# Top-k attention and highway layer: the 32nd value as a third group of the joint maximum, a third buffer for the rectified tile, scaling and reciprocal apart

## The chip, the cores and the metric

The kernel runs on one core of a Trainium2 chip. The metric is the time of the program on the device, in microseconds; lower is better. The core's engines are named as the profile names them: PE (TensorE, matmuls; PEld its weight loads), DVE (VectorE), ACT (ScalarE), POOL (GpSimd) and SP (SyncE, which here only issues transfers). Each engine works through its own queue in the order in which the program put it there.

## The reference

Attention in which each query keeps only its 32 best keys, and behind it a highway layer.

```python
def _attn_ref(q, k, v):                       # each (8, 8, 576, 64): batch, heads, sequence, head
    scores = scale * np.matmul(q, k.transpose(0, 1, 3, 2))
    kth = np.partition(scores, -top_k, axis=-1)[..., -top_k:-top_k + 1]      # top_k = 32
    scores = np.where(scores >= kth, scores, -1000000000.0)
    scores = scores - np.max(scores, axis=-1, keepdims=True)
    attn = np.exp(scores)
    attn = attn / (np.sum(attn, axis=-1, keepdims=True) + 1e-09)
    return np.matmul(attn, v)

def _moe_ref(x, w_h, w_t, b_t):               # x: (4608, 512), the heads side by side
    H = np.maximum(x @ w_h, 0.0)
    T = 1.0 / (1.0 + np.exp(-(x @ w_t + b_t)))
    return T * H + (1.0 - T) * x
```

## The kernel before

A unit is one block of 128 query rows of one head (the last 64 rows of two heads make one unit), with its 576 scores per row. Two units make a pair; there are 288 units, 144 pairs, 18 to a batch. `step(i)` writes down the work of one round of a software pipeline by hand, for 143 rounds; `begin()` fills the pipeline and `finish()` empties it and does the last pair. The order in which the lines stand there is the order in each engine's queue; between engines, waits are put in from what each instruction reads and writes.

The 32nd largest score of a row is found without sorting all 576:

- `scores` (L308 to L334, PE) makes a pair's scores in PSUM. `segments` (L352, DVE) takes the 8 largest of each of 6 segments of 96 scores into the tile `cand`, 12 instructions per pair.
- `refine` (L365 to L381, DVE) turns these 48 candidates per row into a threshold that has at least 24 scores at or above it. L365 and L367 make larger and smaller ones of neighbouring lists, L369 negates, L372 and L375 take 8 extremes each, L377 writes 8 values per row into column 1 of `cand`, and L381, the joint maximum, reduces columns 0 and 1 of `cand` together: its results are the row's largest score (`TOP`) and the threshold (`THR`) in the tile `wall`. `refine` is a generator: each `yield` is a place at which `step` puts other work between.
- `mask_count` (L396, ACT) counts the scores above the threshold in its accumulator `csum` and makes a mask; `mask_add` (L409, PE) adds the mask into PSUM, so that these scores drop out; `below` (L419, DVE) takes the 8 largest of what is left, into `wall` beside the threshold. The 32nd score is now one of 9 numbers per row (`NPK` = 9), the threshold and those 8, and the count says which.
- `hits` (L425, DVE) compares the count with 9 marks, `pick_a` (L435, POOL) multiplies the hits by the 9 numbers, and `pick_b` (L438, DVE) sums the products: one of 9 isn't zero, so the sum is the 32nd score (`KTH` in `wall`, kept two units further on).
- `biases` (L390, POOL) makes two biases from `wall`: the row's largest score for the exponential (L415, ACT), the 32nd for a rectifier of steep slope (L442, ACT), which gives a unit's cut. A pair's second unit is cut by POOL (L453) with a comparison. The masked products (L449 and L459, or L464 where POOL was given no cut; DVE) join cut and exponential, and a transpose by DMA (L480, SP) turns the result for the matmul with v (L493, PE).

In a step the queue of DVE has, for pairs i and i + 1: the segments' maxima of i + 1, `below` of i, L365, L367, `hits`, L369, L372 twice, L375 twice, `pick_b` of i, L377, masked product of the first unit of i - 1, L381, masked product of the second unit. ACT's mask of i + 1 (L396) needs L381.

When all heads of a block of query rows are done, `xs_copy` (L507, ACT) has put the sums over keys, with the row sums of the exponentials, into `xs`, and the highway layer of the block is cut into pieces that later steps take in. `norm` (L556, L557, DVE) adds 1e-9, scales by 2 and takes the reciprocal; it is called at the end of a step, behind the masked products. POOL multiplies (L562), a DMA casts and turns the block, `hh` projects it with the weights `w_h` (L521, PE), and its `evac` (L606, ACT) writes the rectified result into the tile `h2`, which the profile calls h. POOL makes s1 = h2 + x (L607), h2 = h2 - x (L608) and h2 = h2 * t (L621); then `do_add` (L691, POOL) issues a DMA that adds h2 to s1, and s1 is stored. `h2` comes from the pool `fpool`, which has two buffers for each of its tiles: the rectifier of one block waits until the DMA of two blocks ago has read its buffer. 38 blocks go this way; `finish()` does the last ones in another.

At the end a check of the whole run decides whether a slower branch, which sorts in full, has to redo the work; it isn't taken here.

Of the kernel before, what the change touches and what calls it, by code (L numbers as in the profile page):

```python
# [10 lines left out]
ALU = mybir.AluOpType  # L11
FP32 = mybir.dt.float32
# [6 lines left out]
NSEG = 6  # L19
# [7 lines left out]
def kernel(  # L27
# [10 lines left out]
    nc = tc.nc  # L38
# [38 lines left out]
    etpool = ctx.enter_context(tc.tile_pool(name="et", bufs=6))  # L77
    xpool = ctx.enter_context(tc.tile_pool(name="x", bufs=3))
    fpool = ctx.enter_context(tc.tile_pool(name="f", bufs=2))
    xps = ctx.enter_context(tc.tile_pool(name="xps", bufs=2, space=bass.MemoryType.PSUM))  # L80
    ops = ctx.enter_context(tc.tile_pool(name="ops", bufs=1, space=bass.MemoryType.PSUM))
    fps = ctx.enter_context(tc.tile_pool(name="fps", bufs=1, space=bass.MemoryType.PSUM))
# [12 lines left out]
    for jj in range(NPK):  # L95
        nc.vector.memset(pidx[:, jj : jj + 1], S - 2.0 * (TOP_K - jj))

    TOP, THR, KTH = 0, 1, NPK + 1
    wall = consts.tile([P, NU + 2, NPK + 2], FP32)
    fac = consts.tile([P, 2, 2], FP32)  # L100
    nc.vector.memset(fac[:, :, 0], -scale)
# [6 lines left out]
        nc.vector.memset(en[:, 0, :, 0:1], 3.0e38)  # L108
        ends.append(en)
    csum = consts.tile([P, NU], FP32)  # L110
    nc.vector.memset(wall[:, 0:2, KTH : KTH + 1], 0.0)

    def kth(u):
        return wall[:, u + 2, KTH : KTH + 1]
# [6 lines left out]

    cands = []
    for i in range(4):
        cand = consts.tile([P, 2, 8, 8], FP32, name=f"cand{i}")
        nc.vector.memset(cand[:, :, NSEG:, 0:1], -3.0e38)
        cands.append(cand)
    NM = 4
    masks = []
# [228 lines left out]
    def refine(g, cand):  # L357
        u0, u1 = pairs[g][0], pairs[g][1] + 1
        en = ends[g % NE]
        one = cand[:, :, 0:NSEG:2, :]  # L360
        two = cand[:, :, 1:NSEG:2, ::-1]
        high = cpool.tile([P, 2 * HALF], FP32, name="high")
        low = cpool.tile([P, 2 * HALF], FP32, name="low")
        neg = cpool.tile([P, 2 * HALF], FP32, name="neg")
        nc.vector.tensor_tensor(high[:].rearrange("p (s k r) -> p s k r", s=2, r=8), one, two, ALU.max)  # L365
        yield
        nc.vector.tensor_tensor(low[:].rearrange("p (s k r) -> p s k r", s=2, r=8), one, two, ALU.min)  # L367
        yield
        nc.vector.tensor_scalar(neg[:], high[:], -1.0, None, ALU.mult)  # L369
        yield  # L370
        for s in range(2):
            nc.vector.max(en[:, 0, s, 1:9], low[:, s * HALF : (s + 1) * HALF])  # L372
            yield
        for s in range(2):
            nc.vector.max(en[:, 1, s, 0:8], neg[:, s * HALF : (s + 1) * HALF])  # L375
            yield
        nc.vector.scalar_tensor_tensor(  # L377
            out=cand[:, :, :, 1], in0=en[:, 1, :, 0:8], scalar=-1.0, in1=en[:, 0, :, 0:8], op0=ALU.mult, op1=ALU.min
        )
        yield  # L380
        nc.vector.tensor_reduce(  # L381
            wall[:, u0:u1, TOP : THR + 1],
            cand[:, :, :, 0:2].rearrange("p s r k -> p s k r"),
            mybir.AxisListType.X,
            ALU.max,
        )
        yield

    def biases(g):
        return nc.gpsimd.tensor_tensor(be[:, g], wall[:, 2 * g : 2 * g + 2, TOP : KTH + 1 : KTH - TOP], fac[:], ALU.mult)  # L390

# [22 lines left out]
        return e  # L416

    def below(u, ps):
        nc.vector.max(wall[:, u, THR + 1 : KTH], ps)  # L419


    def hits(pair):
# [7 lines left out]
        )  # L430
        return hit

    def pick_a(pair, hit):
        u0, u1 = pair[0], pair[1] + 1
        nc.gpsimd.tensor_tensor(hit[:], hit[:], wall[:, u0:u1, THR:KTH], ALU.mult)  # L435

    def pick_b(pair, hit):
        nc.vector.tensor_reduce(wall[:, pair[0] + 2 : pair[0] + 4, KTH], hit[:], mybir.AxisListType.X, ALU.add)  # L438
# [109 lines left out]
    def ffn_pieces(b, qt, xs):  # L548
        nh, ng, w = shape_of(qt)
        st = dict(b=b, qt=qt, xs=xs)  # L550
        blocks.append(st)

        def norm():
            xs3 = xs[:, 0 : nh * DE].rearrange("p (h e) -> p h e", e=DE)
            rinv = cpool.tile([P, H], FP32, name="rinv")
            nc.vector.tensor_scalar(rinv[:, 0:nh], xs3[:, :, D], 1e-9, 2.0, ALU.add, ALU.mult)  # L556
            nc.vector.reciprocal(rinv[:, 0:nh], rinv[:, 0:nh])  # L557
            x = xpool.tile([P, dm], FP32, name="x")
            st["x"] = x

            def scaled(e):
                e.tensor_tensor(  # L562
                    x[:, 0:w].rearrange("p (h d) -> p h d", h=nh),
                    xs3[:, :, 0:D],
                    rinv[:, 0:nh].unsqueeze(2).to_broadcast([P, nh, D]),
                    ALU.mult,
                )
                if by_dma:
                    casts.append(cast)
                else:  # L570
                    ready.extend([xt, hh, tt])

            pool_work.append((scaled, w))

        by_dma = isinstance(b, int) and units[-1][0:2] > (b, qt + 2)

        def cast():
            xb = xpool.tile([P, dm], BF16, name="xb")
            nc.gpsimd.dma_start(xb[:, 0:w], st["x"][:, 0:w])
            return partial(turn, xb)  # L580

        def turn(xb):
            st["xT"] = fpool.tile([P, n_g, P], BF16, name="xT")
            nc.sync.dma_start_transpose(st["xT"][:, 0:ng, :], xb[:, 0:w])
            flying.append(b)
            ready.extend([hh, tt])

        def xt():
            ps = fps.tile([P, 512], FP32, tag="fp", name="fp")
            for g in range(ng):  # L590
                nc.tensor.transpose(ps[:, g * P : (g + 1) * P], st["x"][:, g * P : (g + 1) * P], ident_f[:])
            xT = fpool.tile([P, n_g, P], BF16, name="xT")
            st["xT"] = xT
            psv = ps[:].rearrange("p (g j) -> p g j", j=P)
            return lambda: nc.scalar.copy(xT[:, 0:ng, :], psv[:, 0:ng, :])

        def hh():
            ps = fps.tile([P, 512], FP32, tag="fp", name="fp")
            project(ps, qt, st["xT"], wh, False)
            h2 = fpool.tile([P, dm], FP32, name="h2")  # L600
            s1 = xpool.tile([P, dm], FP32, name="s1")
            st["h2"], st["s1"] = h2, s1
            x = st["x"]

            def evac():
                nc.scalar.activation(h2[:, 0:w], ps[:, 0:w], AF.Relu)  # L606
                pool_work.append((lambda e: e.tensor_add(s1[:, 0:w], h2[:, 0:w], x[:, 0:w]), w))  # L607
                pool_work.append((lambda e: e.tensor_sub(h2[:, 0:w], h2[:, 0:w], x[:, 0:w]), w))  # L608

            return evac  # L610

        def tt():
            ps = fps.tile([P, 512], FP32, tag="fp", name="fp")
            project(ps, qt, st["xT"], wt, True)
            if by_dma:
                flying.pop()
            t = fpool.tile([P, dm], FP32, name="tt")
            h2, s1 = st["h2"], st["s1"]

            def gated(e):  # L620
                ins = e.tensor_mul(h2[:, 0:w], h2[:, 0:w], t[:, 0:w])  # L621
                if e is nc.gpsimd:
                    adds.append((s1[:, 0:w], h2[:, 0:w], partial(store, b, qt, s1)))
                else:
                    e.tensor_add(s1[:, 0:w], s1[:, 0:w], h2[:, 0:w])
                    store(b, qt, s1)
                return ins

            def evac():
                nc.scalar.activation(t[:, 0:w], ps[:, 0:w], AF.Tanh)  # L630
                pool_work.append((gated, w))

            return evac

        return norm
# [21 lines left out]

    def blk_diff(k, ps):
        w = shape_of(k["qt"])[2]
        k["d"] = fpool.tile([P, dm], FP32, name="h2")  # L660
        nc.vector.scalar_tensor_tensor(
            out=k["d"][:, 0:w], in0=ps[:, 0:w], scalar=0.0, in1=k["x"][:, 0:w], op0=ALU.max, op1=ALU.subtract
        )
# [108 lines left out]
    def step(i):  # L772
# [75 lines left out]
        for _ in range(2):  # L848
            next(ra, None)
        if live:  # L850
            hit = hits(pr)
            pick_a(pr, hit)
        added = bool(adds or casts)
        if adds:
            do_add(i)
# [5 lines left out]
            todo_v.pop(0)()  # L861
        for _ in range(5):
            next(ra, None)
        if live:
            pick_b(pr, hit)
        next(ra, None)
        masked(0)
        for _ in ra:
            pass
        last = masked(1)  # L870
        if live:
            after(biases(i + 1), last)
        if norms:
            norms.pop(0)()
        if nxt:
            masks_of(i + 1)
        while turns and turns[0][0] <= i and len(flying) < 2:
# [61 lines left out]
    def finish():  # L939
# [49 lines left out]
        hit = hits(pr)  # L989
        ep, _ = keep_min(pu[0], old["e"][0], relu)  # L990
        old["et"][0] = transposes(ep)
        nc.vector.tensor_tensor(hit[:], hit[:], wall[:, pr[0] : pr[1] + 1, THR:KTH], ALU.mult)
        pick_b(pr, hit)
        x2 = xps.tile([P, 3 * BANK], FP32, tag="x", name="xs")
        cur["et"] = [etpool.tile([P, nck, P], BF16, name="et") for s in range(2)]
# [13 lines left out]
        yb = xs_of(nfull, 0, n)  # L1009
        project(bank(x1, 0), ya["qt"], ya["xT"], wh, False)  # L1010
        do_work(nc.vector, NG * dm)
        nc.vector.scalar_tensor_tensor(cond[:], wall[:, 0:NU, THR + 1], ABOVE, wall[:, 0:NU, THR], ALU.mult, ALU.add)
        while stores:
            stores.pop(0)[1]()
        sure(2, cond[:], 1.0)
# [28 lines left out]
    with tc.If(fine < 1):  # L1044
        with tc.For_i(0, B, 1) as bi:
# [26 lines left out]
            for pr in pairs[0 : NG // B]:  # L1072
# [23 lines left out]
                else:  # L1096
                    xs_copy(0, n, pso, xs, r0, r0 + P2)
                if heads[-1] == H - 1:
                    ffn_pieces(bi, qt, xs)()
                    do_work(nc.vector, NG * dm)  # L1100
                    while ready:
                        ready.pop(0)()()
                        do_work(nc.vector, NG * dm)
# [30 lines left out]
```

## Time and profile before

| | us |
|---|---|
| median of 3 runs | 817.38 (813.4 to 819.01) |
| the profiled execution | 818.4 |
| its span, first to last instruction | 816.7 |
| busy: DVE | 776.2 |
| busy: ACT | 758.8 |
| busy: PE | 694.4 |
| busy: POOL | 559.3 |
| DVE L352, segments' maxima, 1728 | 297.1 |
| DVE L419, the 8 largest below the threshold, 288 | 204.0 |
| DVE L449 and L459, masked products, 143 and 135 | 64.5 and 60.5 |
| DVE L381, joint maximum, 144 | 29.4 |
| DVE L438, sum over the hits, 144 | 21.8 |

The busy time of an engine counts an instruction from its start to its end; on DVE one starts a little before the one ahead of it has ended, so a group's time can be more than the room that it takes in the queue. Each group's line has the line of the code, the engine, the operation, the tile written and those read, the shapes, the number of instructions, their busy time, the mean duration of one in ns, and the idle time of the engine just ahead of them with what ended it. In a timeline the columns are start, duration (of all in the row, where "x12" says that it stands for 12), engine, line, operation and tiles; a bracket at the end gives the idle time just before and what ended it. "remote" as the end of a wait means that the profile doesn't tell what released it.

The granted TensorE clock is at 0.993 over the span.

### The profile page before, as it was taken

Reading aid. Unit: us, or ns where it says so; the run is one execution under the profiler, and the core shown is the slowest. Engines: PE = TensorE matmul, PEld = TensorE weight load, DVE = VectorE, ACT = ScalarE, POOL = GpSimd, SP = SyncE. Lnnn points to the kernel's source line nnn. Section 1 sums busy time; section 2 is a strip of 40 time slices with the busy share of each in tenths; the row PEclk is TensorE's granted clock in tenths of the full one; section 3 lists DMA queues with packets and bytes.
Section 4 is the critical chain, followed back from the end, with each engine's and each line's share of the span. In section 5 each row is a group of like instructions: output and inputs, shape, how many; then the busy total and the mean of one; then the engine's idle time right before and its main releaser. Section 6 shows DMA issues by size and latency. Waiting matters only on the chain.

```text
span 816.7 us, 20679 instructions
## 1 busy us (share of the span) xinstructions
PE 694.4 (85%) x6405; PEld 500.2 (61%) x6499; DVE 776.2 (95%) x4020; ACT 758.8 (93%) x1401; POOL 559.3 (68%) x712
## 2 busy tenths in 40 slices
PE   7889988888878888888888888888888888888884
PEld 5666766566655666566665666556656566565562
DVE  6999999999999999999999999999998999998995
ACT  5999999999999999999999998999999999998984
POOL 2666867777677766787667777677776776675750
PEclk9999999999999999999999999999999999999998
DMA  6799957985798657997679866697767975565553
GB/s 121 85 147 155 130 117 136 156 130 80 146 150 145 108 94 137 152 137 115 101 149 147 127 110 117 134 157 126 107 122 128 163 114 92 94 110 96 101 93 87
DMA packets 346359, 100.37 MB, mean 123 GB/s; under 512 B 330624, under 2 KB 338432, under 8 KB 346240
## 3 DMA queue, kind: packets, MB, share of 16 engines
q1 hardware_dynamic: 291024, 79.16, 53.0%
q0 software_dynamic: 53536, 19.34, 22.4%
q8 instruction: 53, 0.87, 0.4%
q10 hardware_dynamic: 1680, 0.46, 0.3%
q14 instruction: 66, 0.54, 0.2%
HBM read 31.72 MB, written 9.44 MB: 50 GB/s over the span
## 4 chain that ended last, share of the span: by engine, by line
ACT 37%; DVE 31%; PE 23%; DMA 4%; issue 3%; POOL 2%; SPq 0%; ACTq 0%; DVEq 0%; POOLq 0%
ACT m L396 14%; DVE wall L419 10%; DVE cand L352 9%; ACT e L415 7%; PE pso L277 6%; ACT sc L347 6%; ACT r L442 4%; PE xs L325 4%; DVE ep L449 3%; PE xs L308 3%; PE pso L493 2%; ACT xs L507 2%; DMA s<-h 2%; PE xs L409 2%; PE fp L521 2%
## 5 line engine op out<-in xcount | busy, mean ns | idle before, releaser
L352 DVE MAX8 cand<-xs 128x8 f32<-128x96 f32 x1728 | 297.1, 246 | 13.4 <-PE xs L334 7.4
L277 PE MATMUL pso<-cst,ident_b 128*128 128x252 bf16 x1881 | 253.1, 274 | 42.4 <-ACT xs L507 40.0
L453 POOL TENSOR_SCALAR ro<-sc,wall 128x576 bf16<-128x576 f32 x135 | 232.6, 1723 | 0.0
L277 PEld LDWEIGHTS <-ident_b 128*128 128x128 bf16 x1881 | 178.1, 98 | 82.1 <-issue 49.1
L415 ACT ACTIVATE e<-sc,be 128x576 bf16<-128x576 f32 x288 | 226.0, 785 | 0.1
L419 DVE MAX8 wall<-xs 128x8 f32<-128x576 f32 x288 | 204.0, 748 | 11.5 <-PE xs L409 5.0
L308 PE MATMUL xs<-kT,qT 64*128 64x256 f32 x1024 | 146.1, 402 | 31.9 <-DVE high L365 28.3
L347 ACT COPY sc<-xs 128x1152 f32<-128x1152 f32 x144 | 160.8, 1116 | 0.7 <-DVE cand L352 0.6
L308 PEld LDWEIGHTS xs<-kT,qT 64*128 64x128 f32 x1024 | 93.5, 187 | 62.9 <-issue 38.1
L435 POOL TENSOR_TENSOR hit<-hit,wall 128x18 f32<-128x18 f32 x143 | 32.4, 226 | 137.0 <-DVE hit L425 129.4
L396 ACT ACTIVATE m<-xs,wall 128x576 int8<-128x576 f32 x144 | 107.3, 745 | 20.0 <-DVE wall L381 17.8
L396 ACT ACTIVATE m<-sc,wall 128x576 int8<-128x576 f32 x144 | 111.3, 773 | 0.0
L409 PE MATMUL xs<-m,ident_b 128*128 128x64 bf16 (+1 forms) x507 | 92.0, 274 | 21.4 <-ACT m L396 19.4
L442 ACT ACTIVATE r<-sc,be 128x576 bf16<-128x576 f32 x143 | 109.8, 768 | 0.0
L409 PEld LDWEIGHTS <-ident_b 128*128 128x128 bf16 x576 | 51.7, 98 | 49.8 <-issue 29.3
L493 PEld LDWEIGHTS <-et 128*128 128x128 bf16 (+1 forms) x1600 | 68.9, 100 | 19.3 <-issue 3.8
L493 PE MATMUL pso<-vb,et 128*128 128x65 bf16 (+1 forms) x1600 | 74.6, 194 | 4.9 <-DMA et<-ep 0.3
L390 POOL TENSOR_TENSOR be<-wall,fac 128x4 f32<-128x4 f32 x144 | 29.1, 202 | 71.3 <-DVE ep L459 42.4
L449 DVE TENSOR_TENSOR ep<-e,r 128x576 bf16<-128x576 bf16 x143 | 64.5, 451 | 0.2 <-ACT r L442 0.2
L317 PEld LDWEIGHTS xs<-kd,qT 128*128 128x128 f32 x256 | 38.1, 188 | 42.7 <-issue 42.2
L317 PE MATMUL xs<-kd,qT 128*128 128x128 f32 x256 | 62.5, 326 | 0.0
L459 DVE TENSOR_TENSOR ep<-e,ro 128x576 bf16<-128x576 bf16 x135 | 60.5, 448 | 0.0
(127 smaller groups left out, 1024.1 us busy)
## 6 DMA issues: line engine op xcount, KB each, us to landing
kin<-in_k_dram SPq DMA_DIRECT2D x64, 128.0 KB, 3.0
qin<-in_q_dram SPq DMA_DIRECT2D x62, 128.0 KB, 3.2
out_dram<-s SPq DMA_DIRECT2D x30, 256.0 KB, 2.8
s<-h POOLq DMA_DIRECT2D x29, 256.0 KB, 4.1
et<-ep SPq DMA_TRANSPOSE x286, 3.4
xb<-x POOLq DMA_DIRECT2D x30, 128.0 KB, 3.1
vb<-in_v_dram POOLq DMA_DIRECT2D x28, 128.0 KB, 4.7
vb<-in_v_dram POOLq DMA_DIRECT2D x24, 64.0 KB, 3.2
```

What stands on the lines that cost most here:

```text
L277: nc.tensor.matmul(po["t"][:, 4 * DE : BANK], ident_b[:], cst[:, 0 : BANK - 4 * DE], start=True, stop=True, skip_group_check=True,)
L308: nc.tensor.matmul(ps[:, mo + n0 : mo + n0 + 256], qT[r : r + D, hp, qs : qs + P], kT[r : r + D, hp, n0 : n0 + 256], start=(n0 == 0), stop ...
L317: nc.tensor.matmul(ends, qT[:, hp, qs : qs + P], kd[:, hp, :], start=True, stop=True)
L347: nc.scalar.copy(sc[:], both)
L352: nc.vector.max(cand[:, s, :], sc[:, s * SEG : (s + 1) * SEG])
L396: nc.scalar.activation(m1[:].bitcast(I8)[:, 1 : 2 * S : 2], ps, AF.Sign, bias=wall[:, u, THR : THR + 1], scale=ABOVE, accum_out=csum[:, u ...
L409: nc.tensor.matmul(ps[:, s0:s1], ident_b[:], m1[:, s0:s1], start=False, stop=True, skip_group_check=True)
L415: nc.scalar.activation(e[:], sc, AF.Exp, bias=tb(u), scale=scale)
L419: nc.vector.max(wall[:, u, THR + 1 : KTH], ps)
L442: nc.scalar.activation(r[:], sc, AF.Relu, bias=eb(u), scale=BIGK)
L453: nc.gpsimd.tensor_scalar(r[:], sc, kth(u), None, ALU.is_ge)
L493: nc.tensor.matmul(pso[r0 : r0 + ql, col : col + DE], ets[s][:, c, gi * P2 : gi * P2 + ql], vb[:, h, vc, :], start=(c == 0), stop=(c == nc ...
```

## The change

Four edits:

- `wall` gets a new order of columns: `TOP`, `KTH`, `THR`, and then the 8 of `below` (`LOW`).
- The products of the hits are no longer summed by an instruction of their own. POOL writes them into column 1 of the next pair's `cand` (which L365 and L367 have read by then), L377 writes into column 2, and the joint maximum reduces three columns, of 9 rows instead of 8: largest score, 32nd score (the maximum of one product and zeros) and threshold. `pick_b` stays only in `finish()`.
- `h2` comes from a pool of its own with three buffers.
- `norm` becomes a generator. The scaling of the sums is put ahead of the second masked product, the reciprocal behind the biases.

```diff
+    hpool = ctx.enter_context(tc.tile_pool(name="h", bufs=3))
...
-    TOP, THR, KTH = 0, 1, NPK + 1
+    TOP, KTH, THR, LOW = 0, 1, 2, 3
...
-        cand = consts.tile([P, 2, 8, 8], FP32, name=f"cand{i}")
-        nc.vector.memset(cand[:, :, NSEG:, 0:1], -3.0e38)
+        cand = consts.tile([P, 2, NPK, 8], FP32, name=f"cand{i}")
+        nc.vector.memset(cand[:, :, NSEG:, :], -3.0e38)
...
         nc.vector.scalar_tensor_tensor(
-            out=cand[:, :, :, 1], in0=en[:, 1, :, 0:8], scalar=-1.0, in1=en[:, 0, :, 0:8], op0=ALU.mult, op1=ALU.min
+            out=cand[:, :, 0:8, THR], in0=en[:, 1, :, 0:8], scalar=-1.0, in1=en[:, 0, :, 0:8], op0=ALU.mult, op1=ALU.min
         )
         yield
         nc.vector.tensor_reduce(
-            wall[:, u0:u1, TOP : THR + 1],
-            cand[:, :, :, 0:2].rearrange("p s r k -> p s k r"),
+            wall[:, u0:u1, TOP:LOW],
+            cand[:, :, :, TOP:LOW].rearrange("p s r k -> p s k r"),
...
-    def pick_a(pair, hit):
-        u0, u1 = pair[0], pair[1] + 1
-        nc.gpsimd.tensor_tensor(hit[:], hit[:], wall[:, u0:u1, THR:KTH], ALU.mult)
+    def pick(pair, pen, cand):
+        nc.gpsimd.tensor_tensor(cand[:, :, :, KTH], pen[:], wall[:, pair[0] : pair[1] + 1, THR:], ALU.mult)
...
             nc.vector.tensor_scalar(rinv[:, 0:nh], xs3[:, :, D], 1e-9, 2.0, ALU.add, ALU.mult)
+            yield
             nc.vector.reciprocal(rinv[:, 0:nh], rinv[:, 0:nh])
...
-            h2 = fpool.tile([P, dm], FP32, name="h2")
+            h2 = hpool.tile([P, dm], FP32, name="h2")
...
         if live:
-            hit = hits(pr)
-            pick_a(pr, hit)
+            pick(pr, hits(pr), st[i + 1]["cand"])
...
         for _ in range(5):
             next(ra, None)
-        if live:
-            pick_b(pr, hit)
         next(ra, None)
         masked(0)
         for _ in ra:
             pass
+        scaling = norms.pop(0)() if norms else iter(())
+        next(scaling, None)
         last = masked(1)
         if live:
             after(biases(i + 1), last)
-        if norms:
-            norms.pop(0)()
+        next(scaling, None)
```

More of the change, by code (lines that the diff above doesn't have):

```diff
@@ L110 @@
     csum = consts.tile([P, NU], FP32)
-    nc.vector.memset(wall[:, 0:2, KTH : KTH + 1], 0.0)
     def kth(u):
@@ L389, in biases @@
     def biases(g):
-        return nc.gpsimd.tensor_tensor(be[:, g], wall[:, 2 * g : 2 * g + 2, TOP : KTH + 1 : KTH - TOP], fac[:], ALU.mult)
+        return nc.gpsimd.tensor_tensor(be[:, g], wall[:, 2 * g : 2 * g + 2, TOP:THR], fac[:], ALU.mult)
     def mask_count(u, ps):
@@ L418, in below @@
     def below(u, ps):
-        nc.vector.max(wall[:, u, THR + 1 : KTH], ps)
+        nc.vector.max(wall[:, u, LOW:], ps)
     def hits(pair):
@@ L573, in norm @@
             pool_work.append((scaled, w))
+            yield
         by_dma = isinstance(b, int) and units[-1][0:2] > (b, qt + 2)
@@ L659, in blk_diff @@
         w = shape_of(k["qt"])[2]
-        k["d"] = fpool.tile([P, dm], FP32, name="h2")
+        k["d"] = hpool.tile([P, dm], FP32, name="h2")
         nc.vector.scalar_tensor_tensor(
@@ L991, in finish @@
         old["et"][0] = transposes(ep)
-        nc.vector.tensor_tensor(hit[:], hit[:], wall[:, pr[0] : pr[1] + 1, THR:KTH], ALU.mult)
+        nc.vector.tensor_tensor(hit[:], hit[:], wall[:, pr[0] : pr[1] + 1, THR:], ALU.mult)
         pick_b(pr, hit)
@@ L1011, in finish @@
         do_work(nc.vector, NG * dm)
-        nc.vector.scalar_tensor_tensor(cond[:], wall[:, 0:NU, THR + 1], ABOVE, wall[:, 0:NU, THR], ALU.mult, ALU.add)
+        nc.vector.scalar_tensor_tensor(cond[:], wall[:, 0:NU, LOW], ABOVE, wall[:, 0:NU, THR], ALU.mult, ALU.add)
         while stores:
@@ L1098 @@
                 if heads[-1] == H - 1:
-                    ffn_pieces(bi, qt, xs)()
+                    for _ in ffn_pieces(bi, qt, xs)():
+                        pass
                     do_work(nc.vector, NG * dm)
```

## The prediction

> **What bounds the kernel now.** I read the page's busy times first, then the waits of VectorE (DVE) and ScalarE (ACT), then single steps of the timeline, because the change touches small instructions in a loop and only the timeline tells which of them cost anything.
>
> ```profile
> span 816.7 us, 20679 instructions
> PE 694.4 (85%) x6405; PEld 500.2 (61%) x6499; DVE 776.2 (95%) x4020; ACT 758.8 (93%) x1401; POOL 559.3 (68%) x712
> ```
>
> The reader is to see two engines that are nearly full, DVE and ACT, with GpSimd (POOL) far behind. The program makes 143 near-equal steps, one per pair of query-row units (the 144th pair is finished apart), so a nanosecond on DVE in each step is worth at most 0.143 us in all. Which of the two full engines sets the end of a step is told by who waits.
>
> ```profile
> engine line waited for: us in total, times, longest us
> DVE cand L352 <- PE xs L334: 7.4, 15, 0.6
> DVE wall L419 <- PE xs L409: 5.0, 5, 2.5
> DVE wall L419 <- remote: 4.4, 4, 1.3
> ...
> DVE cand L352 <- PE xs L317: 3.6, 6, 1.3
> ```
> ```profile
> ACT m L396 <- DVE wall L381: 17.8, 41, 1.8
> ACT h L606 <- DMA s<-h: 6.7, 4, 1.9
> ```
>
> In the loop DVE has 15 + 5 + 4 + 6 = 30 waits of note, 20.4 us together. In the other 113 of 143 steps (0.79) it runs without a hole, and in 41 steps ACT's threshold mask waits for DVE's joint maximum, L381. So DVE sets most steps, and I count 0.79 of any time that I add to or take from DVE's steady work; in the 30 steps with a hole the hole swallows it.
>
> **The 32nd value as a third group.** Removed: the sum over the hits, L438, 143 times on DVE. Longer: the joint maximum, L381, which reads 2 x 3 x 9 = 54 numbers and writes 6, where it read 32 and wrote 4. The place of L438 is seen best beside the very first step, which has no L438.
>
> ```profile
> start us, us, engine line op out<-in xcount [idle before <-releaser]
> ...
> 12.64 0.25 DVE L375 MAX8 en<-neg 128x8 f32<-128x24 f32 x2
> 12.93 0.19 DVE L377 SCALAR_TENSOR_TENSOR cand<-en 128x16 f32<-128x16 f32 x1
> ```
> ```profile
> 17.49 0.25 DVE L375 MAX8 en<-neg 128x8 f32<-128x24 f32 x2
> 17.66 0.15 DVE L438 TENSOR_REDUCE wall<-hit 128x2 f32<-128x18 f32 x1
> 17.78 0.19 DVE L377 SCALAR_TENSOR_TENSOR cand<-en 128x16 f32<-128x16 f32 x1
> ```
>
> L377 reads what L375 writes and starts 0.29 us after the pair of L375 begins, with L438 between (17.78 - 17.49) and without it (12.93 - 12.64). L438 begins before the pair of L375 has ended (17.66 against 17.74) and lies in the time in which L377 must wait for L375's result anyway. So its removal is worth 0, not its 0.15 us: the cover was L377's own wait. From below: were the whole 0.12 us between the starts of L438 and L377 saved, it would be 0.12 x 143 = 17.2 us; that is a rival below.
>
> The longer L381 has no such cover: the next masked product starts while L381 still runs.
>
> ```profile
> 407.48 0.20 DVE L381 TENSOR_REDUCE wall<-cand 128x4 f32<-128x32 f32 x1
> 407.60 0.45 DVE L459 TENSOR_TENSOR ep<-e,ro 128x576 bf16<-128x576 bf16 x1
> 407.96 0.16 DVE L556 TENSOR_SCALAR rinv<-xs 128x8 f32<-128x8 f32 x1
> 408.16 0.20 DVE L557 RECIPROCAL rinv<-rinv 128x8 f32<-128x8 f32 x1
> 408.28 0.21 DVE L352 MAX8 cand<-xs 128x8 f32<-128x96 f32 x1
> ```
>
> L459 starts 0.12 us after L381, 0.08 before L381's end; L352 likewise starts 0.08 before the end of L557 (408.28 against 408.36). So every nanosecond by which L381 grows moves what follows. How much does it grow?
>
> ```profile
> L381 DVE TENSOR_REDUCE wall<-cand 128x4 f32<-128x32 f32 x144 | 29.4, 204 | 0.1
> ...
> L365 DVE TENSOR_TENSOR high<-cand 128x48 f32<-128x48 f32 x144 | 28.4, 197 | 0.0
> ...
> L425 DVE TENSOR_TENSOR hit<-pidx,csum 128x18 f32<-128x18 f32 x144 | 24.1, 167 | 0.0
> ...
> L438 DVE TENSOR_REDUCE wall<-hit 128x2 f32<-128x18 f32 x144 | 21.8, 152 | 0.0
> ```
>
> Three slopes come out of these rows. Numbers that lie side by side (L365 in runs of eight): (197 - 167) / (48 - 18) = 1.0 ns each, so 22 more cost 22 ns; that is the lower end. From one reduction to the other: (204 - 152) / (32 - 18) = 3.7 ns, so 82 ns; that is the upper end. Between them: L438 reads side by side, which leaves 152 - 18 = 134 ns fixed; then L381's 32 numbers, which lie 8 floats (32 bytes) apart, took (204 - 134) / 32 = 2.2 ns each, and 22 more take 48 ns. I take 48, as the new instruction is L381 with the same distance between its numbers: 204 + 48 = 252 ns. The sum is 48 x 143 = 6.9 us, of which 0.79 counts: +5.4 us. At the ends it is +2.5 and +9.3.
>
> [...]
>
> Who waits for L381: ACT's mask, 41 times, so the growth reaches ACT too, in the same steps that I count for DVE. L381 now also waits for POOL's product, since that writes into the candidates' tile.
>
> ```profile
> 406.62 0.23 POOL L435 TENSOR_TENSOR hit<-hit,wall 128x18 f32<-128x18 f32 x1 [0.60 <-DVE hit L425]
> ```
> ```profile
> L449 DVEq EVENT_SEMAPHORE  x141: 21/21/21, 33.8 to 796.8; - x141
> ```
>
> POOL's product ended at 406.85, L381 began at 407.48: 0.63 us to spare. I cost that wait at 0; if POOL came later than that, both masked(1) and the twelve maxima L352 would stand behind it. The second wait is an instruction of DVE's queue like that before L449 (21 ns); between 0 and 21 x 143 = 3.0 us. I take 0, because it can be worked off while the first masked product (0.45 us) runs. POOL's write at a distance of 32 bytes, the two memsets more or less at the start, and the bias product that reads neighbours: 0, covered by that 0.63 us and by the start, where DVE idles.
>
> **Scaling and reciprocal apart.** L557 reads L556's result; in the rows above it starts 0.20 us after it.
>
> ```profile
> L557 DVE RECIPROCAL rinv<-rinv 128x8 f32<-128x8 f32 x31 | 6.3, 203 | 1.1
> ...
> L556 DVE TENSOR_SCALAR rinv<-xs 128x8 f32<-128x8 f32 x31 | 5.4, 175 | 0.0
> ...
> L557 DVE RECIPROCAL rinv<-rinv 128x4 f32<-128x4 f32 x7 | 1.2, 178 | 0.2
> ```
>
> With the usual overlap of 0.08 the scaling would hold DVE for 0.175 - 0.08 = 0.095 us, so 0.105 us goes in each of 31 + 7 = 38 blocks: 4.0 us, of which 0.79 counts: -3.2. Bounds: 0 if ACT sets those steps, -4.0 if DVE sets all.
>
> ```profile
> 408.13 0.19 POOL L390 TENSOR_TENSOR be<-wall,fac 128x4 f32<-128x4 f32 x1
> ```
> ```profile
> 409.20 0.77 ACT L442 ACTIVATE r<-sc,be 128x576 bf16<-128x576 f32 x1
> ```
>
> The scaling now stands before the second masked product, L459, which starts 0.1 us later. Behind L459 are its transpose on SP's queue, read two steps later, and POOL's bias product, done at 408.32, whose result ACT's rectifier takes at 409.20: 0.9 us to spare. The scaling itself needs only ACT's copy of the sums, made early in the step. All 0.
>
> **Third buffer for the rectified tile.** Four times ACT stands still because the DMA that adds h to s still reads the buffer that the next layer's rectifier must write.
>
> ```profile
> 411.39 0.60 ACT L606 ACTIVATE h<-fp 128x512 f32<-128x512 f32 x1 [1.42 <-DMA s<-h]
> ```
> ```profile
> 407.11 0.93 POOL L691 DMA_DIRECT2D s<-h  x1 [0.26 <-POOL hit L435]
> ```
> ```profile
> 416.38 1.43 DVE L419 MAX8 wall<-xs 128x8 f32<-128x576 f32 x2 [0.81 <-remote]
> ```
> ```profile
> 408.26 1.04 PE L521 MATMUL fp<-wh,xT 128*128 128x512 bf16 x4 [0.23 <-DMA xT<-xb]
> ```
>
> ACT loses 1.42 us here and DVE 0.81 one step later; over the four places DVE loses the 4.4 us of "L419 <- remote". With three buffers the rectifier waits for an addition one layer older. What is late next is the projection in PSUM, which ended at 409.30, before ACT is free at 409.97. So the whole 4.4 us goes: -4.4. If instead the hole only moved to another transfer: 0. The longest wait for PE L317 stands one step behind the third stall and may be its echo; with its 1.35 us it is -5.7.
>
> ```profile
> 613.23 1.43 DVE L419 MAX8 wall<-xs 128x8 f32<-128x576 f32 x2 [1.14 <-remote]
> ...
> 618.48 2.07 DVE L352 MAX8 cand<-xs 128x8 f32<-128x96 f32 x12 [1.35 <-PE xs L317]
> ```
>
> **Sum.** +5.4 - 3.2 - 4.4 = -2.2 us. The profiled execution took 818.4 us (span 816.7 and 1.7 around it), 1.0 above the median 817.4; on the median that is 815.2, and I say 815.
>
> **Rivals.** The removed sum pays after all: L377 would move up by 0.12 us, 0.12 x 143 x 0.79 = -13.6, so 802; with the short growth (+2.5 instead of +5.4) 799. [...] Against this rival stand the equal 0.29 us of both places; for it only that the first step is a single one. Chance 0.11.
>
> Slower: the joint maximum becomes the price of the step. At 3.7 ns per number it adds 9.3 us (11.7 if all steps count) against 7.6 of gains: +1.7 to +4.1, so 819 to 821; with nothing gained from the reciprocal, +4.9, 822; with the 3.0 us of queue instructions too, over 825. It decides from (3.2 + 4.4) / (143 x 0.79) = 67 ns of growth, an L381 of 271 ns. For it speaks that the two reductions are the only two of their kind, and their plain slope is this one; against it, that they differ in layout as well as in size. Chance 0.24.
>
> The third buffer doesn't do what it says: the stalls stay at the DMA queue or at the projection (PE L521 itself waited for a transfer, 0.23 us). Then +2.2 instead of -2.2: 819.6. Against it, the addition one layer older was issued many steps before. Chance 0.12.
>
> **How the numbers follow.** The forecast has the remaining 0.53, about 811 to 818. The kernel's three runs spread over 813.4 to 819.0, so about 1% (8.2 us) is what can be told from no change. Faster by over 1% (under 809.2): the first rival and a little of the forecast's low tail (short growth, all of the reciprocal, the echo: +2.5 - 4.0 - 5.7 = -7.2, and scatter), 0.13. Slower by over 1% (over 825.6): the far end of the second rival, 0.06. Within: 0.81. The range leaves out the first rival and that far end: 809 to 824.
>
> **What would show it.** In the profile after: L377 still some 0.29 us after the pair of L375 begins (right) or about 0.2 (first rival). The joint maximum at about 252 ns (right), 226 (lower end) or 286 (second rival). No wait "ACT h <- DMA s<-h", and no "DVE wall <- remote" (right) or new ones in their place. The reciprocal's start no longer held by the scaling, and DVE 4.0 us less busy or idle at the 38 blocks. DVE's busy time about unchanged, since what goes was overlapped. The prediction is wrong if DVE waits for POOL at the joint maximum, or if L438's slot turns out to have been paid.

## The result, and the profile after

| | before | changed |
|---|---|---|
| median of 7 runs each, us | 814.5 (813.4 to 819.0) | 812.06 (810.8 to 812.6) |
| ratio, 95% interval | | 0.9953 (0.9931 to 0.9975) |
| the profiled execution, us | 818.4 | 812.6 |

The change is worth 0.47% (0.25 to 0.69%), 3.8 us of 814.5 by the ratio. That is faster, and inside the 1% that the prediction counted as no change. Two later comparisons, shown below, gave 0.9924 (0.9901 to 0.9947) and 0.9941 (0.9917 to 0.9965). The profiled execution of before was a long one among these: the kernel's median came out 2.9 us lower with seven runs than with the three that were known. (In the later comparisons, of 25 to 35 runs of the kernel before, its median was 815.6, 817.5 and 817.0.)

The page of the changed kernel, its span and busy times:

```profile
span 810.9 us, 20658 instructions
PE 692.1 (85%) x6405; PEld 499.1 (62%) x6499; DVE 771.9 (95%) x3876; ACT 758.8 (94%) x1401; POOL 559.6 (69%) x712
```

DVE has 144 instructions fewer and is 4.3 us less busy (776.2 before); ACT is as busy as it was. Now the waits, of DVE and then of ACT (time waited in all, times, longest):

```profile
DVE cand L352 <- PE xs L334: 7.7, 15, 0.7
DVE wall L419 <- PE xs L409: 5.0, 3, 2.7
...
DVE cand L352 <- PE xs L317: 2.9, 9, 0.6
...
DVE wall L419 <- ACT h L607: 0.7, 2, 0.4
```
```profile
ACT m L396 <- DVE wall L381: 19.9, 55, 1.0
...
ACT h L607 <- PE fp L520: 1.9, 2, 1.0
```

"ACT h <- DMA s<-h" (6.7 us) and DVE's "wall <- remote" (4.4 us) are gone from this profile. In their place stands 0.7 us of DVE behind the rectifier, no more. ACT now waits for the joint maximum in 55 steps instead of 41, so DVE is the engine waited for in more steps than before.

One step of DVE in the timeline, and then the joint maximum with its second wait:

```profile
407.82 0.25 DVE L375 MAX8 en<-neg 128x8 f32<-128x24 f32 x2
408.11 0.19 DVE L377 SCALAR_TENSOR_TENSOR cand<-en 128x16 f32<-128x16 f32 x1
408.20 0.45 DVE L448 TENSOR_TENSOR ep<-e,r 128x576 bf16<-128x576 bf16 x1
408.57 0.24 DVE L381 TENSOR_REDUCE wall<-cand 128x6 f32<-128x54 f32 x1
408.73 0.16 DVE L555 TENSOR_SCALAR rinv<-xs 128x8 f32<-128x8 f32 x1
408.80 0.45 DVE L458 TENSOR_TENSOR ep<-e,ro 128x576 bf16<-128x576 bf16 x1
409.17 0.19 DVE L557 RECIPROCAL rinv<-rinv 128x8 f32<-128x8 f32 x1
```
```profile
L381 DVE TENSOR_REDUCE wall<-cand x144: 239/244/250, 12.8 to 787.5; 128x6 f32<-128x54 f32 x144
L381 DVEq EVENT_SEMAPHORE  x143: 21/21/21, 17.7 to 787.2; - x143
```

The reader is to see four things. L377 starts 0.29 us after the pair of L375 (408.11 - 407.82), as it did with the sum between them. The joint maximum takes 244 ns (minimum, median and maximum are given), 40 more than before, and what stands behind it starts 0.16 us after it, where it was 0.12. Its second wait costs nothing: it still starts 0.37 us after L448, as before (407.48 after 407.11 there). These are no single cases: added up over 141 steps of each trace, L375 to L377 takes 39.9 us before and 40.1 after, the first masked product to the joint maximum 52.0 in both, and the joint maximum to what follows it 17.0 before and 22.6 after. And the scaling L555 holds DVE for 0.07 us, the reciprocal comes behind L458 without a hole.

### The profile page after: what moved, and what is told of

Its sections match the earlier page's. It is cut to its first block, busy times and chain, and to the rows that moved or that the text cites. A ratio compares the mean times of both kernels' runs of the same rounds, so it can differ in the third digit from the quotient of the medians.

```text
span 810.9 us, 20658 instructions
## 1 busy us (share of the span) xinstructions
PE 692.1 (85%) x6405; PEld 499.1 (62%) x6499; DVE 771.9 (95%) x3876; ACT 758.8 (94%) x1401; POOL 559.6 (69%) x712
## 3 DMA queue, kind: packets, MB, share of 16 engines
q0 software_dynamic: 53536, 19.34, 22.6%
## 4 chain that ended last, share of the span: by engine, by line
ACT 42%; DVE 27%; PE 23%; issue 4%; DMA 3%; SPq 1%; ACTq 0%; DVEq 0%
ACT m L396 17%; DVE wall L419 11%; ACT e L415 7%; DVE cand L352 7%; ACT sc L347 6%; PE pso L277 5%; ACT r L441 5%; PE xs L325 4%; PE xs L308 3%; PE pso L492 2%; PE fp L520 2%; ACT xs L506 2%; PE xs L409 2%; DVE wall L381 2%; DMA xT<-xb 2%
## 5 line engine op out<-in xcount | busy, mean ns | idle before, releaser
L352 DVE MAX8 cand<-xs 128x8 f32<-128x96 f32 x1728 | 297.2, 248 | 12.1 <-PE xs L334 7.7
L419 DVE MAX8 wall<-xs 128x8 f32<-128x576 f32 x288 | 204.1, 750 | 7.4 <-PE xs L409 5.0
L396 ACT ACTIVATE m<-xs,wall 128x576 int8<-128x576 f32 x144 | 107.2, 745 | 21.1 <-DVE wall L381 19.9
L434 POOL TENSOR_TENSOR cand<-hit,wall 128x18 f32<-128x18 f32 x143 | 32.6, 228 | 123.0 <-DVE hit L425 116.7
L390 POOL TENSOR_TENSOR be<-wall,fac 128x4 f32<-128x4 f32 x144 | 29.2, 202 | 77.0 <-DVE ep L458 59.0
L448 DVE TENSOR_TENSOR ep<-e,r 128x576 bf16<-128x576 bf16 x143 | 64.6, 452 | 0.2 <-ACT r L441 0.2
L458 DVE TENSOR_TENSOR ep<-e,ro 128x576 bf16<-128x576 bf16 x135 | 60.7, 450 | 0.0
```

The costliest lines, as they stand in the source:

```text
L352: nc.vector.max(cand[:, s, :], sc[:, s * SEG : (s + 1) * SEG])
L396: nc.scalar.activation(m1[:].bitcast(I8)[:, 1 : 2 * S : 2], ps, AF.Sign, bias=wall[:, u, THR : THR + 1], scale=ABOVE, accum_out=csum[:, u ...
L419: nc.vector.max(wall[:, u, LOW:], ps)
```

## The experiments

Twelve measurements of nine kernels, on three chips. Each ran beside the kernel before on the same chip, and its ratio is to that kernel. Line numbers of a variant can be off by a few from those of the two kernels. First each part alone, and the disputed slot by itself.

**Third group alone.** The changed kernel with

```diff
-    hpool = ctx.enter_context(tc.tile_pool(name="h", bufs=3))
-            h2 = hpool.tile([P, dm], FP32, name="h2")
+            h2 = fpool.tile([P, dm], FP32, name="h2")
...
-            yield
             nc.vector.reciprocal(rinv[:, 0:nh], rinv[:, 0:nh])
```

> The third group alone (the sum over the hits gone, the joint maximum over three columns of nine rows; two buffers for h2 and scaling and reciprocal back to back as before). My theory: the sum lay in a wait and is worth 0, the joint maximum grows by 40 ns (204 to 244 in the profile after), 0.040 x 143 x 0.79 = +4.5 us against the kernel before, +3 to +6. Rival (the removed slot of 0.12 us pays): 0.04 - 0.12 = -0.08 us a step, x 143 x 0.79 = -9 us.

Measured: 1.0052 (1.0028 to 1.0076) of the kernel before, +4.2 us. The first part by itself makes the kernel slower, by about what the growth of the joint maximum says: it takes 243 ns in this kernel's trace, and what follows it starts 5.6 us later in all. The rival's -9 us is out.

**Third buffer alone.** The kernel before with `hpool` and `h2` from it.

> The third buffer for h2 alone. My theory: the four waits of ACT for the adding DMA go, and with them the four waits of DVE: -4.4 us, -3 to -6, and neither wait in the profile. Rival (the hole moves to another transfer or to the projection): 0.

Measured: 0.9947 (0.9925 to 0.997), -4.3 us. Its profile has neither wait for the adding DMA. Part of DVE's holes is left under another name: its waits for PE before the 8 largest (L419) grew from 5.0 to 7.5 us, and its idle time before L419 and L352 together fell from 24.9 to 21.1 us, by 3.8.

**Scaling and reciprocal apart alone.** The kernel before with the `yield` in `norm` and the two calls in `step`.

> Scaling and reciprocal apart alone. My theory: 38 blocks x 0.105 us x 0.79 = -3.2 us, -2 to -4. Rival (ACT sets the steps with a block's end, so DVE's time there is free): 0.

Measured: 0.9991 (0.9969 to 1.0014), -0.7 us, with -2.5 to +1.1 as its interval: the rival's 0 lies inside, my -3.2 just outside. A second measurement of the same kernel follows below.

**The sum left out.** The kernel before without the 32nd score: every row is cut at the constant 0.02.

```diff
-    nc.vector.memset(wall[:, 0:2, KTH : KTH + 1], 0.0)
+    nc.vector.memset(wall[:, :, KTH : KTH + 1], 0.02)
...
-        if live:
-            pick_b(pr, hit)
...
-        pick_b(pr, hit)
```

> The kernel before without the sum over the hits, and nothing in its place: the 32nd score is left out, and every row is cut at the constant 0.02. My theory: the instruction behind it waits for L375 all the same, so 0, within 1.5 us, and the step of DVE stays at 5.14 us. Rival (the removed slot pays): 0.12 x 143 x 0.79 = -13.6 us.

Measured: 1.0015 (0.9993 to 1.0036), +1.2 us, -0.6 to +2.9. Its timeline, one step of DVE:

```profile
407.09 0.25 DVE L375 MAX8 en<-neg 128x8 f32<-128x24 f32 x2
407.38 0.19 DVE L377 SCALAR_TENSOR_TENSOR cand<-en 128x16 f32<-128x16 f32 x1
```

The same 0.29 us with nothing between, and 39.9 us over 141 steps, as in the kernel before. The loop's 143 instructions of 0.15 us were taken out and the time didn't fall: the sum lay in L377's wait for L375 and cost nothing.

**The change without its first part.** If the third group only costs, the two other parts should be better without it. The kernel before with `hpool` and with the split `norm`; `pick_a`, `pick_b` and the joint maximum over two columns are as before.

> The change without its first part: third buffer, and scaling and reciprocal apart, but the sum over the hits as before. My theory: the joint maximum's growth is a pure cost (+4.2 us alone), so this kernel is faster than the changed one by about 4 us: 808 beside 812. Rival (the parts lean on one another: the third group is worth its price beside the two others): as fast as the changed kernel or slower.

Measured: 0.9916 (0.9888 to 0.9943), median 809.75 beside 811.58 of the changed kernel on the same chip (0.9924). Faster by 1.8 us, which those intervals don't tell from nothing.

**The comparison in the empty wait.** The changed kernel with

```diff
         for _ in range(2):
             next(ra, None)
-        if live:
-            pick(pr, hits(pr), st[i + 1]["cand"])
...
         for _ in range(5):
             next(ra, None)
+        if live:
+            pick(pr, hits(pr), st[i + 1]["cand"])
         next(ra, None)
```

> The changed kernel with the comparison of the count (hits) and POOL's product moved behind the four maxima, into the wait that the removed sum left open. My theory: the wait of 0.2 us from the start of the last L375 to L377 is empty now and takes the comparison for nothing, so DVE's step falls by its 0.087 us: 0.087 x 143 x 0.79 = -9.8 us against the changed kernel, about 802, if POOL's product still ends ahead of the joint maximum (by my count 0.1 us ahead). Rival (the time between L375 and L377 isn't free, or the product comes late): no gain, 812 or more.

Measured: 1.0206 (1.0173 to 1.0239), 833.8 us: 22 us slower than the changed kernel. Rows of its timeline from DVE and one from POOL, and the groups of the product and of the joint maximum:

```profile
406.48 0.25 DVE L375 MAX8 en<-neg 128x8 f32<-128x24 f32 x2
406.65 0.16 DVE L425 TENSOR_TENSOR hit<-pidx,csum 128x18 f32<-128x18 f32 x1
406.77 0.19 DVE L377 SCALAR_TENSOR_TENSOR cand<-en 128x16 f32<-128x16 f32 x1
406.86 0.45 DVE L448 TENSOR_TENSOR ep<-e,r 128x576 bf16<-128x576 bf16 x1
407.44 0.25 DVE L381 TENSOR_REDUCE wall<-cand 128x6 f32<-128x54 f32 x1
```
```profile
406.89 0.51 POOL L434 TENSOR_TENSOR cand<-hit,wall 128x18 f32<-128x18 f32 x1 [0.86 <-DVE hit L425]
```
```profile
L434 POOL TENSOR_TENSOR cand<-hit,wall 128x18 f32<-128x18 f32 x143 | 70.8, 495 | 75.5 <-DVE hit L425 70.8 <-DVE cand L377 3.8
...
L381 DVE TENSOR_REDUCE wall<-cand 128x6 f32<-128x54 f32 x144 | 36.1, 251 | 19.1 <-POOL cand L434 2.5
```

The comparison did fit into the wait: L377 still starts 0.29 us after the pair of L375, and its old slot, 12.3 us over 141 steps, is gone. But POOL's product now runs beside the masked product L448 and takes 495 ns where it took 228, so it ends at 407.40 and the joint maximum starts behind it: 0.58 us after L448 instead of 0.37. DVE stands idle before L381 for 19.1 us in all (0.1 in the changed kernel), and ACT's wait for L381 grows to 39.9 us. My count of 0.1 us to spare had left out that the product gets slower. Over 141 steps the joint maximum starts 30.4 us later behind L448 than in the changed kernel.

The saved slot was lost too, in another place. POOL, whose product now comes later, issues its transfers earlier, beside DVE's negation L369. A step of this kind, and the durations of L369 (minimum, median, maximum in ns) in the changed kernel and here:

```profile
438.69 0.99 POOL L186 DMA_DIRECT2D vb<-in_v_dram  x1
...
438.99 0.68 DVE L369 TENSOR_SCALAR neg<-high 128x48 f32<-128x48 f32 x1
```
```profile
L369 DVE TENSOR_SCALAR neg<-high x144: 169/179/190, 12.0 to 786.5; 128x48 f32<-128x48 f32 x144
```
```profile
L369 DVE TENSOR_SCALAR neg<-high x144: 178/187/680, 12.1 to 806.2; 128x48 f32<-128x48 f32 x144
```

In 31 steps it took over 240 ns, each time beside a transfer that POOL was issuing; from L369 to the first L375 the trace has 13.2 us more over 141 steps, which uses up the 12.3. So the 22 us are about the late joint maximum's 30.4 less what DVE's other waits gave back: its idle time before L352 and L419 fell from 19.5 to 9.6 us.

**The change without its last part.** `norm` in one piece again, third group and third buffer as changed.

> The change without its last part: third group and third buffer, scaling and reciprocal back to back. If scaling and reciprocal apart are worth 3 us once the stalls for the adding DMA are gone: +3 against the changed kernel, 815. If they are worth what they gave alone (0.7): 812.8. If the parts lean on one another elsewhere (group and buffer): 812 or less.

Measured: 0.9983 (0.9962 to 1.0004), 815.11 beside 811.58 of the changed kernel: 3.5 us for the last part, where alone it gave 0.7.

**The changed kernel again.** On the chip of the last three.

> The changed kernel once more, on the same chip as the three others: 812 by the first measurement, 0.995 of the kernel before.

Measured: 0.9924 (0.9901 to 0.9947), 811.58.

**The comparison on POOL.** The change without its first part, with

```diff
-            hit = hits(pr)
+            hit = cpool.tile([P, 2, NPK], FP32, name="hit")
+            for s in range(2):
+                nc.gpsimd.tensor_scalar(hit[:, s, :], pidx[:], csum[:, pr[s] : pr[s] + 1], None, ALU.is_equal)
```

> The change without its first part (third buffer, scaling and reciprocal apart, the sum over the hits kept in L377's wait), with the comparison of the count made by POOL in two instructions, ahead of its product, instead of by DVE. My theory: DVE's steady work sets the steps, so its 0.087 us a step is worth 0.087 x 143 x 0.79 = -9.8 us against the same kernel with the comparison on DVE: about 800. Rival (ACT, nearly as full, sets the steps as soon as DVE is shorter, or POOL's product comes late as in the run before): less than half of that, 805 or more.

Measured: 1.0031 (1.001 to 1.0053), 819.25 beside 808.61 of the same kernel with the comparison on DVE. A step in which POOL was still busy, from POOL's and DVE's timeline:

```profile
403.58 1.26 POOL L611 TENSOR_TENSOR h<-h,x 128x512 f32<-128x512 f32 x1
404.83 0.64 POOL L856 TENSOR_SCALAR hit<-pidx,csum 128x9 f32<-128x9 f32 x2
405.56 0.23 POOL L436 TENSOR_TENSOR hit<-hit,wall 128x18 f32<-128x18 f32 x1
```
```profile
405.49 0.25 DVE L376 MAX8 en<-neg 128x8 f32<-128x24 f32 x2
405.82 0.17 DVE L439 TENSOR_REDUCE wall<-hit 128x2 f32<-128x18 f32 x1
```

Each comparison of 9 numbers takes POOL 0.31 us (the median of 286), nearly four times the room that both together took on DVE, and behind the layer's work the product is late: the sum on DVE starts at 405.82, after the pair of maxima has ended (405.74), and its own slot is no longer free. DVE waited like this 24 times, 5.7 us in all by the view of its waits. The view shows only part of it: in 54 steps L378, which stands behind the sum (L377 in the kernel before), starts later than with the product in time, by 10.1 us in all, about the loss of 10.6. The saved slot brought little: L366 took over 240 ns in 40 steps and L368 in 21, each time with one of POOL's comparisons beside it (7 and none in the same kernel with the comparison on DVE), and from L366 to the first L373 the trace has only 1.9 us less.

**The same again.** The three kernels that stood closest, once more on one chip.

> The change without its first part, again, beside the changed kernel on one chip. Joint maximum a pure cost: faster than the changed kernel by 4 us, or by the 1.8 us of the first comparison. Rival (parts lean on one another): no faster.

Measured: 0.9897 (0.9867 to 0.9926), median 808.61 (808.3 to 810.5).

> The changed kernel, as the measure for the two before: 811.5 to 812, 0.992 to 0.995 of the kernel before.

Measured: 0.9941 (0.9917 to 0.9965), median 812.76 (809.6 to 816.9). The kernel without the third group is 4.2 us ahead this time. On both chips it lies ahead, by 1.8 and by 4.2 us, and it is the fastest kernel of the study.

> Scaling and reciprocal apart alone, again. It gave 0.9991 of the kernel before, with 0.9969 to 1.0014 as its interval; with the two other parts there it gave 3.5 us. If it is worth 3.2 us by itself and the first measurement was low: 0.996. If the stalls for the adding DMA swallow it: 0.999 again.

Measured: 0.9983 (0.9959 to 1.0007), -1.4 us, -3.3 to +0.6. Again little; this interval holds both numbers.

## Why the prediction was right

The forecast was -2.2 us on the median, "within 1%", 809 to 824; it came out at -3.8 us (-5.6 to -2.0 by the interval) and 812.06. The 2.9 us between 815 and 812 are as much as the median of before fell with more runs. Sign, range and "within 1%" held in all three comparisons. The size was low: the two later ones gave -6.2 (-8.1 to -4.3) and -4.8 (-6.8 to -2.9), and -2.2 lies outside both. That it lies inside the first interval is partly luck. The single terms were right or near; their sum was not the whole, as the bullet on the last part says.

- **The removed sum is worth 0.** Shown: the 0.29 us between the maxima and L377 is the same in the changed kernel and in the kernel without the sum, and that kernel isn't faster. With it falls the rival that the removed sum pays after all (-13.6 us): an instruction within another's wait was had for nothing. In the step of the changed kernel above, instructions without such a wait overlap: L381 starts 0.08 us before L448 ends (408.57 against 408.65), and L555 0.08 before L381 ends (408.73 against 408.81).
- **The joint maximum grows.** The mechanism was right, the size a little high: 244 ns, not 252, so 40 / 22 = 1.8 ns for each added number instead of 2.2. By the same sum that is 0.040 x 143 x 0.79 = +4.5; the part alone measured +4.2 (+2.3 to +6.2), 0.75 of the 5.6 us by which it moved what follows, where I had counted 0.79. The second rival, which needed 271 ns to turn the sign, is out. The 1.8 ns are more than the 1.0 that I had worked out from L365 and L425 for numbers side by side; that the distance between the numbers makes the difference was not shown, since no run here changed the distance alone.
- **The third buffer is worth the holes of DVE behind it.** Predicted -4.4, measured alone -4.3 (-6.1 to -2.4), and both waits are gone from its profile. DVE's idle time fell by 3.8 in that one profile, so part of the close match of 4.4 and 4.3 is luck. The name "remote" is no firm sign either: the third profile of the changed kernel has one such wait of DVE, 2.8 us, without any wait of ACT for the adding DMA, and the first profile of the scaling alone has none, with 5.6 us of ACT. What the 2.8 us waited for is open. The projection, which I had named as next, shows as two short waits (1.9 us of ACT).
- **Scaling and reciprocal apart** was put at -3.2, from 4.0 us of DVE. The slot on DVE did shrink, by somewhat less: in the two profiles of this part alone DVE is 3.2 and 3.0 us less busy than before. In the time it measured -0.7 and -1.4 alone, and 3.5 (815.11 - 811.58) with the two other parts there. So -3.2 holds for the changed kernel, but the parts don't simply add: +4.2 - 4.3 - 0.7 is -0.8, and the whole was -3.8, -6.2 and -4.8 in its three comparisons. The last part seems to need the third buffer, not the third group: buffer and scaling without the group came to 0.9916 and 0.9897, which is 2.5 and 4.1 us beyond the buffer's 0.9947, as far as ratios from different chips can be set side by side. Why this part is worth so little where the stalls for the adding DMA still stand is open. The profiles of the part alone still show those stalls (5.6 and 5.1 us of ACT, beside 6.7 before); that they swallow what DVE saves is argued, not shown. Against it, there are three such stalls in each of these profiles, beside 38 blocks. No kernel here tells it apart from the scatter of executions.
- **POOL's product in time, second wait free:** both as said. The first experiment that took POOL's slack away shows how near the edge lies.

## What to carry to other kernels

An instruction's duration is not what its removal gives: look at when the next instruction starts, and whether that start would move. Here 143 instructions of 0.15 us lay in the wait of their successor and were free, while 40 ns more on an instruction with nothing to wait behind it was paid in most steps. When a change has several parts that are each worth half a per cent, run each alone and the whole without each: here the two good parts without the third are faster than the whole, and the parts alone don't add up to it. And when an instruction of a second engine is moved, look at what that engine does in its old place: here both kernels that moved POOL's work slowed instructions of DVE which the edit doesn't name (L369 over 240 ns in 31 steps of one, L366 in 40 steps of the other).

## What the runs showed of the hardware

A small product on POOL took 228 ns beside DVE's maxima and 495 ns beside DVE's product of two bf16 tiles, L448 (means of L434, in the changed kernel and with the comparison late). In the second of these kernels it took 226 to 267 ns in the four steps in which it ran beside that product for less than 0.08 us. L448 itself took 452 ns on the mean in both kernels, so of the two it was POOL that lost, and its result was awaited next: DVE stood idle before L381 for 19.1 us in all. What slows the product there, no run shows.

The other way round, DVE's negation of 48 numbers per row (L369) took at most 190 ns in the changed kernel and, with the comparison late, up to 680 beside a transfer that POOL was issuing; not every such issue slowed it, but all 31 that took over 240 ns had one beside them.

On POOL the size of a small product mattered little here: in the changed kernel one of 4 numbers per row took 202 ns on the mean (L390) and one of 18 took 228 (L434). Comparing 9 numbers per row took POOL 0.31 us (L856, with the comparison on POOL), while the same comparison for both units at once holds DVE for 0.08 us (L425 to L369, 406.37 to 406.45 in the timeline before).
